# Sliding-window attention and a gated layer on one core: attention rewritten in blocks of 32 queries by 64 keys

## The chip, the core and the metric

One NeuronCore of a Trainium2 chip runs the whole program. Its engines work in parallel and meet through semaphores: TensorE (PE in the profile; PEld are its weight loads) for matmuls and transposes, VectorE (DVE), ScalarE (ACT), GpSimd (POOL), and SyncE (SP), from whose queue all DMA transfers between the large memory and the on-chip buffers are issued. Matmuls write into PSUM; VectorE and ScalarE read it from there. The metric is device time in microseconds (us), the median of several executions.

## What is computed

Eight batch entries, 8 heads, 576 positions, 64 features a head, all fp32. Heads 0 to 3 are "plain" (each query sees the last 32 keys), heads 4 to 7 "dilated" (every fourth key, 32 of them). The attention's output, heads side by side (512 features), goes through a gated layer with a causal convolution over 5 positions.

```python
scores = scale * np.matmul(q, k.transpose(0, 1, 3, 2))
rel = pos[:, None] - pos[None, :]
mask_plain = (rel >= 0) & (rel < 32)
mask_dil = (rel >= 0) & (rel < 32 * 4) & (rel % 4 == 0)
attn = softmax(np.where(mask, scores, -1e9))
x = np.matmul(attn, v)        # heads moved beside each other: [8, 576, 512]
for k in range(5):
    gate_pre += conv_w[k] * xp[:, k:k + S, :]
gate = 1.0 / (1.0 + np.exp(-gate_pre))
out = (gate * (x @ w_val)) @ w_out
```

## The kernel before, in words

**Who sets the order.** Every piece of work is a `Task` with an engine, an assumed duration, the tasks it depends on, and the buffers it needs (`Ten`). `Plan.run` simulates the engines on these durations and emits the instructions in the order it finds: at each step the task that could start first, and among equals the one with the lowest priority number. A batch b has priority b for dilated attention, b + 0.45 for plain, b + `lag` (1.171) for the gated stages; `TUNE["kind"]` shifts each kind. Loads go out strictly in the order of their priorities and wait there for a free buffer. A waiting instruction holds back all that stands behind it on its engine.

**Dilated attention** (`dilated`, heads in two pairs y). One load each brings q and k for the four heads: 96 partitions of 12 rows (3 KB) per head pair (`load_qk`, L340). v comes with 4 positions a partition, twice for some of them: `va` 128 partitions, `vb` the last 64 (L363, L368); GpSimd casts both to bf16 (L386). Six transposes per operand (L548) bring features onto partitions, where two heads lie in the two halves; VectorE and ScalarE evict them (L557, L382, L384). Scores are matmuls of 64 keys by up to 126 queries in quadrants of the array (L577), in two halves cb. The exponential is on ScalarE (L394), the mask multiply on VectorE (L407). Attention times v is 4 matmuls of full height (L588) and 4 of 64 by 32 (L596). A column of ones beside v gives the row sums; the reciprocal (L606) and the multiply (L607) normalise. Transposes (L616, L619) bring the result back, and a copy puts it into `xT` (L382 on ScalarE, L384 on VectorE).

**Plain attention** (`plain`) does the same with 48 transposes of 96 columns per batch (24 for q, 24 for k; L430), score matmuls of 64 keys by 96 queries (L463), attention times v on 128 rows of `et` (L476), normalising (L486, L487) and transposes (L496). Its v is loaded in overlapping windows of 128 rows each 96 rows (L348, L354), in packets of 256 B, so that a third of v is read twice.

**Gated stages** (`gated`) per batch, in two halves of 288 positions and two pairs of chunks: the convolution as 20 matmuls of 64 by 64 with diagonal weights (L647), tanh on ScalarE (L657), the value product as 8 matmuls (L665), and their product on VectorE (L675) into `y_all`. **Outputs**: 36 blocks of 128 rows, each 4 matmuls of 512 columns (L692), an eviction (L700 on ScalarE, L702 on VectorE) and a store (L706).

The weights come through `va` buffers after the first loads (L750); GpSimd casts them (L762, L772). PSUM has three tiles of two banks (`ps2`, shown as pd) and two of one bank (`ps1`, shown as pu).

```python
key = (at, t.prio, s + dur)
if best is None or key < best[0]:
    best = (key, t, eng, dur, s)
```

Of the kernel before, what the change touches and what calls it, by code (L numbers as in the profile page):

```python
# [2 lines left out]

# [8 lines left out]
ALU = mybir.AluOpType  # L12
# [4 lines left out]
TUNE = {'seed': 108242,  # L17
 'jit': 0,
 'lag': 1.171,
 'plain': 0.45,  # L20
 'unit': 0.056,
 'half': 0.406,
 'chunk': 0,
 'look': {'PE': 0.0, 'ACT': 0.081, 'DVE': 0.05, 'POOL': 0.309, 'SP': 0.02},
 'flex': 0.712,
 'switch': 0.047,
 'kind': {'V': 0.708,
          'Sp': -0.063,
          'EXp': 0.259,
          'Y': -0.322,  # L30
          'Td': 0.582,
          'Md': -0.23,
          'Ct': 0.552,
          'Cd': 1.11,
          'Ed': 0.138,
          'Np': -0.673,
          'Qd': -0.751,
          'early': -0.369,
          'Kd': -0.627,
          'Ap': 0.43,  # L40
          'EXd': 0.163,
          'ST': -0.388,
          'EKp': 0.363,
          'Wv': -0.368,
          'Mp': -0.254,
          'Ep': 1.186,
          'Nd': 0.592,
          'Wo': -0.345,
          'Ad': 0.079,
          'TQp': 0.323,  # L50
          'TKp': -0.445,
          'Xp': 0.531,
          'EQp': -0.504,
          'Sd': -0.045,
          'G': -0.497,
          'Xd': -0.432,
          'EO': 0.659,
          'C': 0.303,
          'O': -0.056}}
# [39 lines left out]
class Plan:  # L99
# [15 lines left out]
    def add(self, *a, **k):  # L115
        t = Task(*a, **k)
        kind = t.name.rstrip("0123456789")
# [84 lines left out]
def kernel(  # L202
# [17 lines left out]
    W = 32  # L220
    PB = 12
    NP = S // PB
    TT = S // R
    NCH = Dm // 128
    NB = S // 96
# [4 lines left out]
    PM = 42  # L230
    M1, M2 = 3 * PM, 3 * (NP - PM)
    K1 = TT - 128
    scale = 1.0 / float(D) ** 0.5
    HEADS = [[0, 2], [1, 3], [4, 5], [6, 7]]
    VHEADS = [0, 2, 3, 1, 4, 5, 7, 6]

    N = {"ps2": 3, "ps1": 2, "qk": 8, "vp": 2, "va": 3, "vb": 2, "vab": 2, "vbb": 2,
         "qTp": 1, "kTp": 3, "qTd": 2, "kTd": 2, "et": 4, "xn": 3, "gate": 3, "osb": 5, "avt": 2}
# [10 lines left out]
    qk = tiles("qk", [96, 2, PB * D], FP32)  # L249
    vp = tiles("vp", [128, 4, NB, DA], FP32)  # L250
    va = tiles("va", [128, 4, R * D], FP32)
    vb = tiles("vb", [128, 4, R * D], FP32)
    vab = tiles("vab", [128, 4, R, DA], BF16)
    vbb = tiles("vbb", [128, 4, R, DA], BF16)
    qTp = tiles("qTp", [128, PB, 2, NP], BF16)
    kTp = tiles("kTp", [128, 32 + S], BF16)
    qTd = tiles("qTd", [128, 2, 3, 2, NP], BF16)
    kTd = tiles("kTd", [128, 2, 2, TT], BF16)
    et = tiles("et", [128, 2 * HW + 32], BF16)
    xn = tiles("xn", [128, 6, 2, D], BF16)  # L260
    gate = tiles("gate", [128, 2, HW], BF16)
    osb = tiles("osb", [128, Dm], FP32)
    rec = consts.tile([128, 2, 12], FP32, name="rec")

    xT = consts.tile([128, NCH, B * SB], BF16, name="xT")
    y_all = consts.tile([128, NCH, NTOK], BF16, name="y_all")
    ident = consts.tile([128, 128], BF16, name="ident")
    ident2 = consts.tile([128, D], BF16, name="ident2")
    ident_f = consts.tile([8, 8], FP32, name="ident_f")
    perm_p = consts.tile([96, 96], BF16, name="perm_p")  # L270
    perm_m = consts.tile([M1, M1], BF16, name="perm_m")
    perm_r = consts.tile([128, R, 32], BF16, name="perm_r")
    mask_d = consts.tile([128, HW], BF16, name="mask_d")
    mask_p = consts.tile([128, 96], BF16, name="mask_p")
# [7 lines left out]


    def early():
# [3 lines left out]
        nc.vector.memset(mask_d, 1.0)  # L288
        m1 = mask_d[:, 0:2 * M1].rearrange("p (x s t) -> p x s t", x=2, s=3)
        m2 = mask_d[:, 2 * M1:].rearrange("p (x s t) -> p x s t", x=2, s=3)  # L290
        for m, n, b in ((m1, PM, 0), (m2, NP - PM, M1 - K1)):
            band(m, b, [[0, 2], [1, 3], [3, n]])
        nc.vector.memset(mask_p, 1.0)
        band(mask_p.rearrange("p (r t) -> p r t", r=PB), 32, [[1, PB], [PB, 8]])
        for x in vab + vbb:
            nc.vector.memset(x[:, :, :, D:DA], 1.0)
        for x in et:
            nc.vector.memset(x[:, 2 * HW:], 1.0)
        for x in kTp:
            nc.vector.memset(x[:, 0:32], 0.0)  # L300
        for x in vp:
            nc.vector.memset(x[0:32, :, 0, :], 0.0)
            nc.vector.memset(x[:, :, 1:NB, D:DA], 1.0 - 2.0 ** -9)
            nc.vector.memset(x[32:64, :, 0, D:DA], 1.0 - 2.0 ** -9)
            nc.vector.memset(x[64:128, :, 0, D:DA], 1.0 - 2.0 ** -9)
# [3 lines left out]
        nc.vector.tensor_copy(perm_p.rearrange("p (t r) -> p t r", r=PB),  # L309
                              ident[0:96, 0:96].rearrange("p (r t) -> p t r", r=PB))  # L310
        nc.vector.tensor_copy(perm_m.rearrange("p (t s) -> p t s", s=3),
                              ident[0:M1, 0:M1].rearrange("p (s t) -> p t s", s=3))
        nc.vector.tensor_copy(perm_r, ident.rearrange("p (c n) -> p c n", c=R))
        nc.vector.tensor_copy(
            perm_r[:, :, 32 - M2:].rearrange("p c (t s) -> p c t s", s=3),
            ident.rearrange("p (c n) -> p c n", c=R)[:, :, 32 - M2:].rearrange("p c (s t) -> p c t s", s=3))
        nc.vector.memset(
            xT.rearrange("z c (b t) -> z c b t", b=B)[:, :, :, 0:4], 0.0)

    def band(dst, base, pattern):  # L320
        nc.gpsimd.affine_select(out=dst, in_=dst, compare_op=ALU.is_ge, fill=0.0,
                                base=base, pattern=pattern, channel_multiplier=-1)
        nc.gpsimd.affine_select(out=dst, in_=dst, compare_op=ALU.is_ge, fill=0.0,
                                base=W - 1 - base,
                                pattern=[[-a, n] for a, n in pattern],
                                channel_multiplier=1)
# [9 lines left out]
    def load_qk(src, b, dil, y, ten, prio):  # L336
        ys = range(2) if y is None else [y]

        def issue():
            nc.sync.dma_start(  # L340
                out=qk[ten.idx][:, ys[0]:ys[-1] + 1, :],
                in_=src_ap(src, (b * H + 4 * dil + 2 * ys[0]) * S * D,
                           [[PB * D, 96], [2 * S * D, len(ys)], [1, PB * D]]))
        return load(f"qk{b}{dil}", ten, issue, 0.78 * len(ys), prio)

    def load_vp(b, ten, prio):
        def first():
            nc.sync.dma_start(  # L348
                out=vp[ten.idx][32:128, :, 0, 0:D],
                in_=src_ap(v, b * H * S * D, [[D, 96], [S * D, 4], [1, D]]))  # L350
        res = [load(f"vp{b}", ten, first, 0.43, prio)]
        for h in range(4):
            def rest(h=h):
                nc.sync.dma_start(  # L354
                    out=vp[ten.idx][:, h, 1:NB, 0:D],
                    in_=src_ap(v, (b * H + h) * S * D + 64 * D,
                               [[D, 128], [96 * D, NB - 1], [1, D]]))
            res.append(load(f"vp{b}{h}", ten, rest, 0.72, prio))
        return res

    def load_vd(b, ta, tb, prio):
        def first():
            nc.sync.dma_start(  # L363
                out=va[ta.idx],
                in_=src_ap(v, (b * H + 4) * S * D, [[R * D, 128], [S * D, 4], [1, R * D]]))

        def second():
            nc.sync.dma_start(  # L368
                out=vb[tb.idx][64:128],
                in_=src_ap(v, (b * H + 4) * S * D + (TT - 64) * R * D,  # L370
                           [[R * D, 64], [S * D, 4], [1, R * D]]))
        return (load(f"va{b}", ta, first, 1.5, prio), load(f"vb{b}", tb, second, 0.8, prio))


    def score_mm(o, lhs, rhs, lane):
        for m in range(2):
            nc.tensor.matmul(out=o[64 * m:64 * m + 64], lhsT=lhs[:, 64 * m:64 * m + 64],
# [437 lines left out]
```

## Time and profile before

| | |
|---|---|
| Median of 3 runs | 205.73 us (204.80 to 207.56) |
| The profiled execution's span | 206.9 us |
| PE, VectorE, ScalarE, GpSimd busy | 165.9, 121.0, 102.4, 33.2 us |
| Mean granted clock of TensorE | 0.922 |
| Read from and written to the large memory | 33.30 MB, 9.44 MB |
| DMA packets | 43687, of them 25731 under 512 B |

The profile is one execution; its span is the time from the first to the last instruction, and no other time of that execution is recorded. "Busy" is the union of an engine's instructions. Matmuls are pipelined, so a row's mean duration of one matmul holds latency, and many of them overlap; the time of a group in the chain of waits, or from its start to the next group's start, is a better price. The granted clock is the share of full speed that TensorE was given. A line such as L577 is a line of the kernel's file; where a helper records the instruction, several tiles share a line.

### The profile page before, as it was taken

To read this page: it belongs to the slowest core of one execution; us is meant where nothing else is said; L and a number is where in the kernel's file an instruction comes from. 1 tells how busy PE (TensorE), PEld (TensorE's weight loads), DVE (VectorE), ACT (ScalarE), POOL (GpSimd) and SP (SyncE) were. 2 spreads that over 40 slices of the span, in tenths; PEclk is the share of its full clock that TensorE was granted. 3 is DMA by queue.
4 is the path that set the end of the run, shared out by engine and by line. 5 is a ranking of instruction groups with operands and counts; after the bars stand their busy time and mean duration, and the time that the engine had idled before them with its cause. 6 is when DMAs were issued, how large, how long until landed. Compare 5 with 4: busy or idle time off the path is not lost.

```text
span 206.9 us, 7180 instructions
## 1 busy us (share of the span) xinstructions
PE 165.9 (80%) x3117; PEld 121.9 (59%) x3140; DVE 121.0 (58%) x239; ACT 102.4 (49%) x170; POOL 33.2 (16%) x52
## 2 busy tenths in 40 slices
PE   1278955992898787949995999599996999999992
PEld 1166834662677665637673767387664766676650
DVE  6165651551597775728874668448665577785320
ACT  2315711451657564742482278552674547846443
POOL 5300272400350040004000340440040000000000
PEclk9999998896559999999999799959997999999998
DMA  6999859999999999999999999999998512202205
GB/s 181 238 230 213 200 157 271 260 198 254 309 282 228 245 220 144 228 257 250 300 258 239 288 244 283 223 272 260 242 310 134 208 51 105 106 3 105 101 34 219
DMA packets 43687, 43.20 MB, mean 209 GB/s; under 512 B 25731, under 2 KB 31880, under 8 KB 43656
## 3 DMA queue, kind: packets, MB, share of 16 engines
q1 hardware_dynamic: 43656, 42.75, 85.2%
q8 instruction: 24, 0.39, 0.9%
q14 instruction: 7, 0.06, 0.1%
HBM read 33.30 MB, written 9.44 MB: 207 GB/s over the span
## 4 chain that ended last, share of the span: by engine, by line
PE 61%; DMA 21%; issue 7%; SPq 4%; DVE 3%; ACT 1%; POOL 1%; ACTq 0%; POOLq 0%; DVEq 0%
DMA qk<-in_k_dram 15%; PE pu L692 14%; PE pd L665 13%; PE pd L647 10%; PE pu L548 4%; PE pd L430 3%; DMA va<-in_moe_w_val_dram 3%; PE pd L476 3%; DMA qk<-in_q_dram 3%; PE pd L577 2%; PE pd L588 2%; SPq L354 2%; PE pd L596 2%; PE pd L463 2%; PE pu L496 2%
## 5 line engine op out<-in xcount | busy, mean ns | idle before, releaser
L394 ACT ACTIVATE et<-pd 128x576 bf16<-128x576 f32 x64 | 38.2, 649 | 29.3 <-PE pd L577 16.6
L665 PE MATMUL pd<-xT,w_val 128*128 128x288 bf16 x256 | 38.0, 295 | 0.5 <-DVE xT L384 0.5
L692 PE MATMUL pu<-w_out,y_all 128*128 128x512 bf16 x121 | 33.0, 380 | 2.0 <-issue 1.1
L657 ACT ACTIVATE gate<-pd 128x576 bf16<-128x576 f32 x32 | 20.5, 652 | 22.8 <-PE pd L647 22.8
L675 DVE SCALAR_TENSOR_TENSOR y_all<-gate,pd 128x576 bf16<-128x576 bf16 x32 | 23.8, 750 | 13.7 <-PE pd L665 13.2
L647 PE MATMUL pd<-xT,conv_diag 64*64 64x288 bf16 x640 | 28.6, 328 | 3.6 <-issue 3.1
L548 PE MATMUL pu<-ident,qk 96*128 96x96 bf16 x192 | 16.0, 236 | 17.0 <-DMA qk<-in_q_dram 16.5
L665 PEld LDWEIGHTS <-w_val 128*128 128x128 bf16 x256 | 24.2, 101 | 7.4 <-POOL w_val L762 0.9
L647 PEld LDWEIGHTS <-conv_diag 64*64 64x64 bf16 x640 | 22.0, 124 | 6.7 <-issue 5.0
L548 PEld LDWEIGHTS <-qk 96*128 96x128 bf16 x192 | 12.0, 113 | 20.3 <-DMA qk<-in_q_dram 17.1
L386 POOL CAST vab<-va 128x1024 bf16<-128x1024 f32 x8 | 8.3, 1040 | 95.1 <-DMA va<-in_v_dram 63.7
L382 ACT COPY xT<-pu 128x576 bf16<-128x576 bf16 x20 | 12.8, 642 | 21.5 <-PE pu L619 15.4
L700 ACT ACTIVATE osb<-pu 128x512 f32<-128x512 f32 x26 | 15.5, 598 | 10.9 <-PE pu L692 9.7
L692 PEld LDWEIGHTS <-y_all 128*128 128x128 bf16 x144 | 12.2, 98 | 13.4 <-issue 1.2
L407 DVE TENSOR_TENSOR et<-et,mask_d 128x576 bf16<-128x576 bf16 x32 | 14.9, 469 | 8.8 <-ACT et L394 8.1
L407 DVE TENSOR_TENSOR et<-et,mask_p 128x576 bf16<-128x576 bf16 x29 | 16.0, 560 | 6.2 <-ACT et L394 5.5
L487 DVE TENSOR_TENSOR xn<-pd,rec 96x768 bf16<-96x768 f32 x16 | 15.3, 954 | 0.6
L557 DVE COPY qTd<-pu 128x576 bf16<-128x576 bf16 x16 | 7.2, 453 | 12.2 <-PE pu L548 12.2
L382 ACT COPY kTd<-pu 128x576 bf16<-128x576 bf16 x12 | 7.7, 638 | 13.0 <-PE pu L548 13.0
L463 PE MATMUL pd<-qTp,kTp 64*64 64x96 bf16 x384 | 10.3, 227 | 4.2 <-issue 3.7
L607 DVE TENSOR_TENSOR xn<-pd,rec 128x640 bf16<-128x640 f32 x16 | 13.2, 824 | 0.5
L430 PE MATMUL pd<-ident,qk 96*64 96x96 bf16 x384 | 11.0, 216 | 2.7 <-DMA qk<-in_k_dram 1.4
(62 smaller groups left out, 185.1 us busy)
## 6 DMA issues: line engine op xcount, KB each, us to landing
out_dram<-osb SPq DMA_DIRECT2D x36, 256.0 KB, 4.7
qk<-in_q_dram SPq DMA_DIRECT2D x15, 576.0 KB, 7.7
qk<-in_k_dram SPq DMA_DIRECT2D x15, 576.0 KB, 9.8
vp<-in_v_dram SPq DMA_DIRECT2D x32, 160.0 KB, 7.7
va<-in_v_dram SPq DMA_DIRECT2D x8, 512.0 KB, 9.5
vb<-in_v_dram SPq DMA_DIRECT2D x8, 256.0 KB, 10.0
va<-in_moe_w_val_dram SPq DMA_DIRECT2D x4, 256.0 KB, 7.2
va<-in_moe_w_out_dram SPq DMA_DIRECT2D x4, 256.0 KB, 6.5
```

The source lines that it names most:

```text
L382: nc.scalar.copy(out=out_, in_=in_)
L394: nc.scalar.activation(out=et[e.idx][:, 0:2 * HW].rearrange("p (l n) -> p l n", l=2), in_=ps2[ps.idx][:, :, 0:HW], func=AF.Exp, scale=scale)
L407: nc.vector.tensor_tensor(out=ev, in0=ev, in1=m, op=ALU.mult)
L430: nc.tensor.transpose(out=o[64 * y:64 * y + 64, r // 3, (r % 3) * 96:(r % 3) * 96 + 96], in_=a[:, y, r * D:(r + 1) * D], identity=ident[0: ...
L487: nc.vector.tensor_tensor(out=xn[xt.idx][0:96].rearrange("p (h j) l d -> p h (j l) d", h=2), in0=a[:, :, :, 0:D], in1=rr[:, :, :, None].to ...
L548: nc.tensor.transpose(out=o[:, (cb * 3 + s) * 96:(cb * 3 + s + 1) * 96], in_=a[:, y, c:c + 128], identity=ident[0:96, 0:96])
L647: nc.tensor.matmul(out=ps2[pc.idx][64 * ob:64 * ob + 64, n, 0:HW], lhsT=conv_diag[rb, 2 * cp + n, kk, :], rhs=xT[rb, 2 * cp + n, s:s + HW] ...
L657: nc.scalar.activation(out=gate[g.idx], in_=ps2[pc.idx][:, :, 0:HW], func=AF.Tanh, scale=0.5)
L665: nc.tensor.matmul(out=ps2[pv.idx][:, n, 0:HW], lhsT=w_val[:, mc, c * 128:(c + 1) * 128], rhs=xT[:, mc, c0:c0 + HW], start=(mc == 0), stop ...
L675: nc.vector.scalar_tensor_tensor(out=y_all[:, 2 * cp:2 * cp + 2, t0:t0 + HW], in0=gate[g.idx], scalar=1.0, in1=ps2[pv.idx][:, :, 0:HW], op ...
L692: nc.tensor.matmul(out=ps1[po.idx], lhsT=y_all[:, c, t0:t0 + 128], rhs=w_out[:, c, :], start=(c == 0), stop=(c == NCH - 1))
L700: nc.scalar.activation(out=osb[ob.idx], in_=ps1[po.idx], func=AF.Copy, scale=0.5)
```

## The change

All heads now go through one function, `attend`, for two heads at a time (four units a batch): 18 blocks of 32 queries by 64 keys (the block's own 32 positions and the 32 before them), for two heads 36 score matmuls, one exponential and one mask multiply over 640 columns, 36 products with v of 64 rows by 32 columns of the array, one normalisation. For the dilated heads a position's four phases are treated as four sequences, of which a unit takes two.

Loads: q and k of the plain heads lie over 128 partitions with 9 rows (2304 B) each, those of the dilated heads with 4 rows (1 KB); v is loaded once, plain in rows of 256 B, dilated in 1 KB. Blocks that start in the middle of a 64-row piece need v shifted by 32 partitions. GpSimd makes that copy (`vs`) in four instructions of 32 partitions, and for the dilated heads an unshifted cast (`vn`). Odd blocks read `vp` or `vn`, even ones `vs`. Transposes back write 64-partition halves of PSUM.

`xT` becomes 4 rotating buffers of one batch, `y_all` 3 rotating buffers of two batches. The planner's constants are new: `lag` 4.106, `plain` 0.442, jitter 0.264 on every priority, other shifts per kind (k loads -1.7 to -1.0, v loads +0.5 and -0.6, w_val load at 0.524 + 0.858, w_out load at 5.256 + 1.13), and 9 `qk` buffers. The gated stages and outputs compute the same as before.

```diff
-TUNE = {'seed': 108242,
- 'lag': 1.171,
+TUNE = {'seed': 283419,
+ 'jit': 0.264,
+ 'lag': 4.106,
+ 'wv': 0.524,
+ 'wo': 5.256,
...
-                in_=src_ap(src, (b * H + 4 * dil + 2 * ys[0]) * S * D,
-                           [[PB * D, 96], [2 * S * D, len(ys)], [1, PB * D]]))
+                in_=src_ap(src, b * H * S * D, [[PJ * D, 128], [2 * S * D, 2], [1, PJ * D]]))
...
+            nc.sync.dma_start(out=t[:, 0:4, :], in_=src_ap(src, o, [[RD, 128], [128 * RD, 4], [1, RD]]))
...
+            nc.sync.dma_start(out=t[0:64, 4, :], in_=src_ap(src, o + 512 * RD, [[RD, 64], [1, RD]]))
...
-                    out=vp[ten.idx][:, h, 1:NB, 0:D],
-                    in_=src_ap(v, (b * H + h) * S * D + 64 * D,
-                               [[D, 128], [96 * D, NB - 1], [1, D]]))
+            nc.sync.dma_start(out=vp[ten.idx][:, :, 0:D],
+                              in_=src_ap(v, b * H * S * D, [[D, 128], [128 * D, 18], [1, D]]))
...
+    def attend(name, b, u, s, qt, kt, deps, v_odd, v_even, v_deps, v_tens, prio):
+        ps, e, po, xt = Ten("ps2"), Ten("et"), Ten("ps2"), Ten("xn")
+
+        def sc(eng):
+            for g in range(NG):
+                h, blk = place(g, s)
+                for l in range(2):
+                    rb = slice(64 * l, 64 * l + 64)
+                    nc.tensor.matmul(
+                        out=ps2[ps.idx][64 * h:64 * h + 64, l, 32 * blk:32 * blk + 32],
+                        lhsT=kT[kt.idx][rb, 32 * g:32 * g + 64],
+                        rhs=qT[qt.idx][rb, 32 * g:32 * g + 32], start=True, stop=True)
...
+            nc.scalar.activation(out=et[e.idx], in_=ps2[ps.idx][:, :, 0:EW], func=AF.Exp, scale=scale)
...
+            nc.vector.tensor_tensor(out=et[e.idx], in0=et[e.idx], in1=m, op=ALU.mult)
...
+                        nc.tensor.matmul(
+                            out=ps2[po.idx][32 * c:32 * c + 32, h, n * DA:(n + 1) * DA],
+                            lhsT=et[e.idx][64 * h:64 * h + 64, l, 32 * blk:32 * blk + 32],
+                            rhs=src(p, l)[64 * h:64 * h + 64], start=True, stop=True,
+                            tile_position=(64 * h, 32 * c))
+        t_a = plan.add(f"A{name}", {PE: 0.30}, avm, deps=[t_m] + v_deps, tens=[e, po, xt] + v_tens,
+                       prio=prio, mode="6432")
...
+                if i == 0:
+                    copy(eng, vs[ts.idx][0:32, 1:18, 0:D], vp[tv.idx][96:128, 0:17, 0:D])
+                else:
+                    copy(eng, vs[ts.idx][a:a + 32, 0:18, 0:D], vp[tv.idx][z:z + 32, :, 0:D])
+            sh.append(plan.add(f"W{b}", {POOL: 1.2}, cv, deps=lv, tens=[tv, ts], prio=prio))
...
+                            nc.tensor.transpose(
+                                out=o[64 * y:64 * y + 64, PR * j:PR * j + PR],
+                                in_=a[rb, (y * PJ + j) * D:(y * PJ + j + 1) * D], identity=ident2[rb, :])
...
+        def nat(eng):
+            copy(eng, vn[tn.idx][:, 0:16, 0:D], vd[tv.idx].rearrange("p c (n x) -> p (c n) x", n=R)[:, 0:16])
+            copy(eng, vn[tn.idx][0:64, 16:20, 0:D], vd[tv.idx].rearrange("p c (n x) -> p (c n) x", n=R)[0:64, 16:20])
+        sh.append(plan.add(f"U{b}", {POOL: 1.4}, nat, deps=lv, tens=[tv, tn], prio=prio))
```

More of the change, by code (lines that the diff above doesn't have):

```diff
@@ L2 @@
 from contextlib import ExitStack
+from itertools import takewhile
 import concourse.bass as bass
@@ L14 @@
 PE, ACT, DVE, POOL, SP = "PE", "ACT", "DVE", "POOL", "SP"
-TUNE = {'seed': 108242,
- 'jit': 0,
- 'lag': 1.171,
[L20 to L59, printed above, removed]
+TUNE = {'seed': 283419,
+ 'jit': 0.264,
+ 'lag': 4.106,
+ 'plain': 0.442,
+ 'unit': -0.05,
+ 'half': -0.304,
+ 'chunk': 0.171,
+ 'look': {'PE': 0, 'ACT': 0.014, 'DVE': 0, 'POOL': 0.804, 'SP': 0.792},
+ 'flex': 0.058,
+ 'switch': 0.083,
+ 'conv': 0.109,
+ 'wv': 0.524,
+ 'wo': 5.256,
+ 'bufs': {'ps2': 3,
+          'ps1': 2,
+          'qk': 9,
+          'vp': 2,
+          'vd': 2,
+          'vn': 2,
+          'vs': 4,
+          'qT': 4,
+          'kT': 4,
+          'et': 4,
+          'xn': 4,
+          'gate': 3,
+          'osb': 5,
+          'xT': 4,
+          'yT': 3},
+ 'kind': {'Y': 0.742,
+          'Ap': -5.466,
+          'G': 2.013,
+          'Nd': 2.485,
+          'Fp': -0.2,
+          'Cd': 3.289,
+          'Lwv': 0.858,
+          'Lc': -0.724,
+          'Fd': -1.043,
+          'Sd': 0.441,
+          'EO': 1.34,
+          'Wo': 0.159,
+          'U': -1.299,
+          'Lwo': 1.13,
+          'Xd': -0.142,
+          'Ekd': -4.439,
+          'Md': -0.853,
+          'Ad': -1.988,
+          'Sp': -0.665,
+          'Xp': -1.215,
+          'Lkr': -1.69,
+          'Lvp': -0.616,
+          'Ekp': -1.147,
+          'Ed': 2.938,
+          'Eqd': -0.076,
+          'Wv': -1.214,
+          'Eqp': 1.365,
+          'Ep': -2.267,
+          'Np': -1.538,
+          'Tqp': -0.912,
+          'Lvd': 0.523,
+          'Tqd': -1.554,
+          'early': 1.836,
+          'Lkd': -1.276,
+          'V': -0.187,
+          'Ct': -3.598,
+          'Lkp': -0.958,
+          'ST': -0.371,
+          'Tkd': -0.913,
+          'W': 2.23,
+          'O': 1.356,
+          'Mp': 0.057,
+          'Lqp': -0.49,
+          'Lqd': 0.396,
+          'Tkp': 3.231,
+          'C': -0.141,
+          'Lvr': 0.691,
+          'Lqr': 0.195}}
@@ L611, in dilated @@
-            t_n = plan.add(f"Nd{b}{y}", {DVE: 1.05}, norm, deps=t_av, tens=[po, xt, at], prio=p)
-            def trx(eng, xt=xt, psx=psx):
-                o = ps1[psx.idx].bitcast(BF16)[:, 0:S].rearrange("p (c t) -> p c t", c=R)
-                xx = xn[xt.idx].rearrange("p n x d -> p n (x d)")
-                nc.tensor.matmul(out=o[:, :, TT - 32:TT], lhsT=xx[:, 4, :], rhs=perm_r,
-                                 is_transpose=True, start=True, stop=True)
-                for c in range(R):
-                    nc.tensor.transpose(out=o[:, c, 0:M1], in_=xx[0:M1, c, :], identity=perm_m)
```

585 lines of the change are left out of this document (263 added, 322 removed).

## The prediction, made before the changed kernel was run

> **What bounds the kernel now.** I read the page first (busy shares, slices), then the table of windows, the chain of waits in order of time, and last the rows of single lines. Batch b below is one of the 8 batch entries, "gated" the stages behind attention (conv, val, their product), "output" the last matmul.
>
> ```profile
> span 206.9 us, 7180 instructions
> ...
> PE 165.9 (80%) x3117; PEld 121.9 (59%) x3140; DVE 121.0 (58%) x239; ACT 102.4 (49%) x170; POOL 33.2 (16%) x52
> ...
> PE   1278955992898787949995999599996999999992
> ...
> PEclk9999998896559999999999799959997999999998
> DMA  6999859999999999999999999999998512202205
> ```
>
> The lines of digits are 40 slices of 5.2 us: the transfers (DMA) are full for 31 slices and nearly idle after. So there are two resources near their limit up to 160 us, and one after. The windows give it in numbers (busy us of each engine, then clock, DMA share, GB/s):
>
> ```profile
> 0.00:40.00 40.00, 24.64 (x426) 19.11 (x430) 19.33 (x59) 12.87 (x20) 13.01 (x34) 0.96 0.92 217
> 40.00:160.00 120.00, 99.18 (x2015) 73.81 (x2027) 76.70 (x138) 64.65 (x108) 20.16 (x19) 0.89 1.07 247
> 160.00:207.00 47.00, 42.12 (x700) 28.94 (x699) 25.00 (x44) 24.87 (x42) 0.00 (x0) 0.97 0.28 103
> ```
>
> PE is idle 15.4 us in the first stage, 20.8 in the second, 4.9 in the third: 41.1 of 206.9. The second stage is also where the granted clock is lowest (0.89). The chain (start, duration, what) says what the idle time is made of:
>
> ```profile
> 3.58 8.36 DMA qk<-in_k_dram
> 17.55 6.77 DMA va<-in_moe_w_val_dram
> 45.11 7.55 DMA qk<-in_k_dram
> 63.60 1.14 PE pd L430 x48
> 67.18 14.86 DMA qk<-in_k_dram
> 85.02 0.45 PE pd L577 x28
> 86.72 0.38 PE pd L463 x24
> 87.71 3.12 issue
> 94.03 0.48 PE pd L476 x12
> 146.80 0.36 PE pu L548 x6
> ```
>
> Between 45 and 82 us two k loads stand on the chain for 22.4 us. Elsewhere PE work of 0.4 to 2 us hands over to PE work. So: PE's own work is the bound, and late loads add to it. The PE rows also price small matmuls: 48 transposes take 1.14 us, 24 score matmuls 0.38, 12 attention-times-v matmuls 0.48.
>
> The last view is that of the mask multiply and of the GpSimd casts (minimum/median/maximum ns):
>
> ```profile
> L407 DVE TENSOR_TENSOR et<-et,mask_d x32: 443/458/925, 7.6 to 178.7; 128x576 bf16<-128x576 bf16 x32
> L407 DVE TENSOR_TENSOR et<-et,mask_p x29: 445/458/1373, 21.0 to 187.0; 128x576 bf16<-128x576 bf16 x29
> ...
> L386 POOL CAST vab<-va x8: 1038/1040/1043, 8.6 to 152.3; 128x1024 bf16<-128x1024 f32 x8
> L386 POOL CAST vbb<-vb x8: 1041/1042/1266, 9.8 to 153.4; 64x1024 bf16<-64x1024 f32 x8
> ```
>
> A mask takes 458 ns, and up to 1373 where it meets a GpSimd instruction.
>
> **The change part by part.** The sum is made against the profiled execution's span, 206.9 us; it is 1.2 us (0.6%) above the median 205.73, inside 204.80 to 207.56.
>
> Transfers. Read bytes go from 33.30 MB to q, k, v once (3 x 9.44) and weights 2.10: 30.4 MB. Writes stay 9.44. By the trace's packets, time over 16 engines: 6144 of 3072 B at 198 ns (76.0 us), 6149 of 1024 B at 73 (27.9), 23572 of 256 B at 25 (36.2), 5632 of 2048 B at 98 (34.5), semaphores 1.6, instructions 2.1; sum 178. After: 4096 of 2304 B (plain q and k, 128 partitions), 13824 of 1024 B, 18432 of 256 B, the same 2048 B. A 2304 B packet over 128 partitions is not in the trace. At the rate of 3072 B over 96 it is 149 ns, at that of the 2048 B stores in the tail (86 ns) it is 97; I take 120, nearer the loads. The 1024 B packets took 58 to 74 ns into 128 partitions (va, batch by batch) and 78 to 98 into 64 (vb); I take 65. Sum 30.7 + 56.2 + 28.8 + 34.5 + 3.7 = 154 us; bounds 142 and 170. Less the stores (26) and the weights (8), that is 120 us for 8 batches: one lands each 15 us.
>
> PE. Gated and output are unchanged: per batch 4 x (0.61 + 0.98), and 36 outputs of 4 x 0.216, 82 us in all at full clock. Attention per batch before, from the chain's and timeline's rows: plain transposes 1.14, dilated 4 x 0.36, scores 2 x 0.38 + 2 x 0.45, attention times v 2 x 0.49 + 4 x 0.40, back transposes 2 x 0.36 + 2 x 0.50: 8.5 us. With 82 that is 150, and 150/0.92 (mean clock) 163, against 165.9 busy: the rows add up. After, per batch:
> - Plain transposes: 72 of 64 columns in place of 48 of 96. L430 runs at 21.4 ns each; scaled by columns 14.3. So 1.0 to 1.5, I take 1.25.
> - Dilated transposes: 20 in place of 24, 128 columns in place of 96: 1.2 to 1.44, I take 1.44.
> - Scores: 144 (32 queries by 64 keys) in place of 112. L463 and L577 run at 14 to 16 ns with their tails, 10.7 without; the 18-column half of L577 gains less than its columns. 1.5 (10.7) to 3.1 (21.4, the start to start of L430, where two halves of the array take turns), I take 2.0 by L577.
> - Attention times v: 144 of 64 x 32 in place of 56. L596, the one 64 x 32 form, starts every 14 ns: 2.0; low 1.5, high 3.1 by the same two rows.
> - Back transposes: 60 of 128 to 64 in place of 22: at 54 ns for 128 columns, two at a time, 0.35 x 2 + 0.62 x 2 = 1.9; 1.65 to 2.4.
> Sum 8.6, low 6.9, high 11.5. Against 8.5 that is nothing; bounds -13 and +24 us over 8 batches. More instructions, but smaller and packed. The term in the sum is 0.
>
> [...]
>
> ScalarE and VectorE. Exponentials: 64 x 649 ns to 32 of 640 columns, 721 ns: -15 us. Masks 64 to 32, 509 each: 31 to 16. Normalising: 32 x (824 + 219) against 35.6: -2. Copies out of PSUM: 88 (54 us) to 96 at some 0.62: +6. The two stand at 223 us of 414 before and at some 198 after. They are off the path; the term is 0. Score tiles leave PSUM sooner: 16 pairs of banks per batch in place of 22.
>
> GpSimd. Per batch: four shifted copies of plain v (3 x 1152 and 1088 elements a partition), four of dilated v (3 x 1024 and 1280) and an unshifted cast (1280), 10.2 k elements at 1.016 ns (the 1024 in 1040 ns): 10.3 us, 83 over the kernel, where 17.0 were. No row moves data between partitions: the low end is this row, the high end 2.1 ns per element (the select of L323, 1.21 us for 576), 21.4 us per batch. I take the cast, which is the same operation. Its cover is PE's pace, (8.6 + 6.4)/0.92 = 16 us per batch. The attention-times-v step waits for it now, and behind that wait on PE stand the next tasks in program order.
>
> Masks against GpSimd. The 61 masks lost 3.3 us over 458 ns while GpSimd was 16% busy: 0.34 us each per full share. With GpSimd at 0.75 in the loading stage that is 0.26 each, 8 us on VectorE, which brings the two engines to 206: hidden, bounds 0 and 32 x 1.0.
> [...]
>
> Order. q and k loads, the weights and stores all pass through SP: 9 loads a batch in place of 11. k is loaded ahead of q by some 1.7 batches, so the first complete batch comes after some 2.9 MB, at about 15 us (plain scores were at 19.7). w_val comes after some 2.4 batches, cast at about 42 us (28.6 before); w_out after some 6.6 batches, near 105 us, where the first output ran at 40.2. Outputs are held until then: six batches of y have buffers, and it is the same 34 us of PE work, done later, while reads have the queue alone. I cost this at 0 in the sum, but if w_out were later than 120 us the 31 us of outputs and the last gated work would not be covered by any attention. At the start I take idle 17 in place of 15.4: +1.5.
>
> Where the stall goes. Idle in 40 to 160 was 20.8. A batch lands each 15 us and takes PE 16, so most waits for k go; the next late things are v's copies and the exponential behind a score. I leave 9 of 20.8: -12 (bounds -19 and 0). Clock: 0.71 in 40 to 60 and 0.84 in 120 to 140 lost 4 + 3 us; half comes back with the gaps gone: -3.5 (0 to -7). Tail: the same 3.6 us after the last matmul.
>
> Sum: 206.9 + 0 - 12 - 3.5 + 1.5 = 193; on the scale of the median 192.
>
> **The rivals.**
> First, cheaper small matmuls: attention at the low end, 6.9 per batch, takes 13 more: 179. For: L463 unstalled at 10.7 ns. Against: tails of 0.1 to 0.2 us at each change of shape, as L588 to L596.
> Second, the loads gain and PE gives it back: attention at 10.0 per batch, half way to the high end, is +12: 204. For: twice the small matmuls. Against: L596's 14 ns.
> Third, GpSimd becomes the bound, the other side. Place: the attention-times-v step of each half batch. It starts near 14 us, needs 8 x, 6 us of weights, then the last batch's attention and gated work (16) and the end (4). At 2.1 ns per element x is 21.4: 211. It decides from x = 19 us (1.87 ns per element). [...] Against: both casts at 1.04 us.
> Fourth, attention at the high end, small matmuls at L430's 21.4 ns: +24: 216. For: successive score blocks share a quadrant. Against: 10.7 to 16 ns in the rows of quadrant matmuls. [...]
>
> **How the numbers follow.** Forecast 0.46 (183 to 201 by itself), first rival 0.16, second 0.15, third 0.13, fourth 0.10. 2% is about what a measurement of this kernel can tell: under 201.6 is faster, over 209.8 slower. Faster: nearly all of the forecast, the first, a fifth of the second: 0.64. Same: the rest of the forecast and most of the second: 0.10. Slower: third, fourth, a fifth of the second: 0.26. The range 174 to 216 leaves out the lowest of the first, the upper part of the third and half of the fourth, some 0.13.
>
> **What would show it.** Right: DMA time near 154 us (share 0.8 of a 192 us span) with reads done by 130; PE busy 160 to 168; idle in the middle under 10; GpSimd some 90 busy, a copy of 1024 at 1.04; masks mostly over 0.51 until the loads end; outputs only after about 105 us. Wrong: a shifted copy over 1.9 us, PE waiting for GpSimd on the chain; scores of 36 over 0.7 us; DMA share unchanged.

## The result, and the profile after

The changed kernel takes 234.35 us (median of 4 runs, 231.01 to 236.04) where the kernel before took 206.64 beside it on the same chip (204.80 to 210.45): a ratio of 1.125, 95% interval 1.110 to 1.140. The forecast was 192 (174 to 216). The profiled execution of the changed kernel took 236.04 us with a span of 234.3; it is one of the longer ones (the shortest took 231.01), and the accounting below is of it.

Page of the changed kernel: busy shares, slices of 5.9 us, queues.

```profile
span 234.3 us, 10001 instructions
...
PE 176.4 (75%) x4564; PEld 130.1 (56%) x4564; DVE 107.4 (46%) x210; ACT 98.6 (42%) x159; POOL 91.3 (39%) x107
...
PE   0352747898695958984795699099789889999993
PEclk9999999999978897999589779769999999999999
DMA  4999999844977930399009897502004404614155
...
q1 hardware_dynamic: 43880, 39.86, 57.6%
q8 instruction: 35, 0.57, 1.0%
```

The loads need less, as was forecast: the row of transfers, full for 31 slices before, has holes from the ninth slice on. VectorE, ScalarE and GpSimd are all under half busy. And yet PE is busy for a smaller share (75% where it was 80%), with holes that no other row fills. The windows of the changed kernel put numbers to it (busy of each engine, clock, DMA share, GB/s):

```profile
0.00:40.00 40.00, 17.43 (x573) 14.02 (x577) 21.13 (x66) 11.02 (x17) 20.59 (x39) 1.00 0.98 265
40.00:160.00 120.00, 92.38 (x2778) 73.01 (x2771) 60.47 (x101) 50.55 (x82) 69.85 (x68) 0.87 0.61 170
160.00:234.30 74.30, 66.62 (x1221) 43.10 (x1219) 25.76 (x44) 37.04 (x61) 0.85 (x1) 1.00 0.34 128
```

PE's idle time in the three stages is 22.6, 27.6 and 7.7 us, against 15.4, 20.8 and 4.9 before: 16.8 more. Its busy time is 10.5 more (176.4 against 165.9). Together that is the 27.4 us between the two spans. The chain of waits of the changed kernel names what the idle time waits for:

```profile
19.61 3.41 issue
31.76 4.74 issue
...
61.07 2.27 issue
...
71.58 2.51 issue
...
83.47 2.72 issue
...
109.20 3.81 issue
...
125.96 2.45 issue
...
146.86 5.72 issue
```

"Issue" is time in which the engine waited for nothing that the profile shows: no semaphore, no transfer of the kernel's, no other engine. It is 17.4% of the chain, the largest entry, where it was 7.1% before (the longest ones are shown). The stop at 109.20 stands in the middle of a task, as the timeline of PE shows (start, time to the end of the last, line, tile, matmuls):

```profile
108.93 0.20 PE L446 MATMUL pd<-vs,et 64*32 64x65 bf16 x2
...
109.01 0.19 PE L446 MATMUL pd<-vn,et 64*32 64x65 bf16 x1
113.01 0.23 PE L446 MATMUL pd<-vn,et 64*32 64x65 bf16 x1 [3.81 <-issue]
113.02 0.24 PE L446 MATMUL pd<-vs,et 64*32 64x65 bf16 x2
```

Some 19 of one task's 36 products start within 0.1 us, PE stands still for 3.8, and the others follow. Both parts read the same tiles, so no tile can have been late. When PE's instructions are counted from the start, matmuls and weight loads together, the stops fall on round numbers. My count of the trace of the changed kernel:

```
stop at us       19.61 27.14 31.76 42.37 61.07 71.58 83.47 109.20 125.96 167.48 190.03
instructions so far 446  702   958  1214  2238  2750  3262   4796   5564   7355   8379
minus 190, / 256      1    2     3     4     8    10    12  17.99  20.99  27.99  31.99
```

(A few records are missing from the trace, hence 17.99.) The queue called "instruction" carries packets of 16384 bytes; 256 instructions lie between two such boundaries, and 35 packets for PE's 9128 instructions fit that. So a packet is 256 instructions; I call it a code page. At 109.20 PE stops, the next packet starts at 110.33 and takes 1.08 us, and PE goes on 1.6 us after its end. Before, PE had 6280 instructions (3140 weight loads and as many matmuls, of which 3117 are in the trace) and 24 packets.

From 19 us on all 17 stops of over 0.5 us stand at such a boundary, 38.5 us in all; in the kernel before 5 do, 10.9 us. (This is my sum over the traces, between the first and the last matmul; "stops for code" below are these.) PE's other gaps fell from 21.8 to 9.9 us, and its busy time rose by 10.5. So the stops for code, 27.6 us more, are as much as the whole loss of 27.4; the other two changes nearly cancel.

The packet list also tells why a page is late. By the stops, a packet brings the page that begins 1.3 to 1.6 us after its end. In the changed kernel 32 of the 35 packets start 1.0 us or more after PE has begun the page before that one (the three others from 0.4 us ahead to 0.8 behind), also after pages that lasted 8 to 15 us and left time to spare. So in this trace code came one page ahead at most: 1.0 us to the packet's start, 1.1 for the packet and 1.4 until PE went on make some 3.5 us from page to page, and a page used up sooner ended in a stop.

### The profile page after: what moved, and what is told of

Its sections match the earlier page's. It is cut to its first block, busy times and chain, and to the rows that moved or that the text cites. A ratio compares the mean times of both kernels' runs of the same rounds, so it can differ in the third digit from the quotient of the medians.

```text
span 234.3 us, 10001 instructions
## 1 busy us (share of the span) xinstructions
PE 176.4 (75%) x4564; PEld 130.1 (56%) x4564; DVE 107.4 (46%) x210; ACT 98.6 (42%) x159; POOL 91.3 (39%) x107
## 4 chain that ended last, share of the span: by engine, by line
PE 70%; issue 17%; DMA 6%; DVE 4%; ACT 1%; SPq 0%; DVEq 0%; ACTq 0%
PE pd L664 15%; PE pu L692 13%; PE pd L646 10%; PE pu L617 7%; PE pu L584 7%; PE pd L419 6%; PE pd L446 5%; PE pu L495 4%; DMA qk<-in_q_dram 4%; PE pu L524 3%; DVE et L431 2%; DMA qk<-in_k_dram 2%; DVE kT L403 1%; DVE yT L674 1%; PE pu L526 0%
## 5 line engine op out<-in xcount | busy, mean ns | idle before, releaser
L405 POOL CAST vs<-vp 32x1152 bf16<-32x1152 f32 (+1 forms) x32 | 36.4, 1141 | 27.0 <-DMA vp<-in_v_dram 25.6
L674 DVE SCALAR_TENSOR_TENSOR yT<-gate,pd 128x576 bf16<-128x576 bf16 x32 | 23.9, 753 | 42.0 <-PE pd L664 42.0
L405 POOL CAST vs<-vd 32x1024 bf16<-32x1024 f32 (+1 forms) x32 | 35.5, 1111 | 1.7
L692 PE MATMUL pu<-w_out,yT 128*128 128x512 bf16 x144 | 33.2, 379 | 0.0
L700 ACT ACTIVATE osb<-pu 128x512 f32<-128x512 f32 x36 | 21.5, 597 | 27.4 <-PE pu L692 27.4
L584 PE MATMUL pu<-ident,qk 128*128 128x128 bf16 (+1 forms) x160 | 19.7, 248 | 9.7 <-DMA qk<-in_k_dram 5.6
L495 PE MATMUL pu<-ident,qk 64*64 64x64 bf16 x576 | 15.7, 209 | 13.2 <-issue 10.4
L426 ACT ACTIVATE et<-pd 128x640 bf16<-128x640 f32 x32 | 21.6, 709 | 7.9 <-PE pd L419 7.8
L431 DVE TENSOR_TENSOR et<-et,mask 128x640 bf16<-128x640 bf16 x32 | 20.8, 670 | 4.3 <-ACT et L426 4.3
L692 PEld LDWEIGHTS <-yT 128*128 128x128 bf16 x144 | 13.8, 97 | 15.3 <-issue 1.4
L495 PEld LDWEIGHTS <-qk 64*64 64x64 bf16 x576 | 13.5, 123 | 14.2 <-issue 12.0
```

Source lines behind the costliest of these rows:

```text
L405: nc.gpsimd.tensor_copy(out_, in_)
L426: nc.scalar.activation(out=et[e.idx], in_=ps2[ps.idx][:, :, 0:EW], func=AF.Exp, scale=scale)
L431: nc.vector.tensor_tensor(out=et[e.idx], in0=et[e.idx], in1=m, op=ALU.mult)
L495: nc.tensor.transpose(out=o[64 * y:64 * y + 64, PR * j:PR * j + PR], in_=a[rb, (y * PJ + j) * D:(y * PJ + j + 1) * D], identity=ident2[rb, :])
L584: nc.tensor.transpose(out=o[:, 128 * c:128 * c + m], in_=a[0:m, c * RD + 128 * cb:c * RD + 128 * cb + 128], identity=ident[0:m, 0:m])
L674: nc.vector.scalar_tensor_tensor(out=yT[yb.idx][:, 2 * cp:2 * cp + 2, t0:t0 + HW], in0=gate[g.idx], scalar=1.0, in1=ps2[pv.idx][:, :, 0:HW ...
```

## The experiments

Theory C: PE waits for its own code. In the changed kernel's trace two packets of code start 3.34 us apart or more, 256 instructions of small matmuls are used up in 1 to 2 us (an estimate from its chain, where the 72 of a unit's products take 0.34 us and those of its scores 0.42), and the change raised PE's instructions from 6280 to 9128. Rivals: L, the loads come late, because the load queue stands behind plain v's buffer (54.5 us in 5 waits on the queue of SP); G, GpSimd's copies hold products up or lengthen the masks on VectorE (482 ns at the median, up to 1537); P, the outputs come too late (the first at 157 us), so that nothing covers their stage. Several kernels leave part of the computation out; the expectations say which. Ratios are to the kernel before.

**The old kernel with more instructions.** Same mathematics, same columns: conv and value matmuls cut in two, the output matmul in four.

```diff
-for kk in range(K):
-    for n in range(2):
-        for hb in range(2):
+for z, kk, n, hb in [(z, kk, n, hb) for z in (0, 144) for kk in range(K)
+                     for n in range(2) for hb in range(2)]:
...
-for mc in range(NCH):
+for z, mc in [(z, mc) for z in (0, 144) for mc in range(NCH)]:
...
-for c in range(NCH):
+for z, c in [(z, c) for z in range(0, 512, 128) for c in range(NCH)]:
```

> The kernel before, same results, but its wide matmuls are cut: convolution and value product in 2 pieces of 144 columns, output in 4 of 128. The array streams the same columns; PE's instructions (matmuls and weight loads) go from 6275 to 8931, about as many as the changed kernel's 9123. Theory C (PE waits for its own code at the end of each page of 256 instructions, 16 KB): 10 more pages; if every page cost what those of the changed kernel cost on average (about 2.3 us beyond cover) this gives 206 + 23 = 229 us; if only pages that are used up faster than the next arrives (some 4 us) cost, then only the convolution's 5 new pages count (128 matmuls of 15 ns, 2 us a page) and it is some 216. Theory L (loads held behind the two buffers of plain v) and theory G (GpSimd's copies): neither is in this kernel, so only the small cost of more matmuls, at most 5 us: 206 to 211.

Measured 233.58 us, ratio 1.124 (1.104 to 1.144). The old loads, the old GpSimd work and the old order of outputs, with 35 packets of code like the changed kernel, give the changed kernel's time. It is 4 us above what C had with every page at the changed kernel's price (229) and far above C's other figure (216, only the convolution's pages). The stops for code grow from 10.9 to some 29 us. The rest of the 26.7 us is not split further; the cut also doubles the weight loads of these matmuls (PEld 159.2 us busy). The page of this kernel:

```profile
span 232.4 us, 9859 instructions
...
PE 176.5 (76%) x4468; PEld 159.2 (69%) x4468; DVE 122.2 (53%) x239; ACT 102.2 (44%) x170; POOL 33.6 (14%) x52
...
q8 instruction: 35, 0.57, 1.1%
```

**The changed kernel with fewer instructions.** Scores in 4 matmuls of 320 columns per unit in place of 36 of 32, products in 8 of 325 in place of 36 of 65; loads, copies, exponentials, masks and outputs as they were.

```diff
-for g in range(NG):
-    h, blk = place(g, s)
+for h in range(2):
...
-        out=ps2[ps.idx][64 * h:64 * h + 64, l, 32 * blk:32 * blk + 32],
+        out=ps2[ps.idx][64 * h:64 * h + 64, l, 0:EW],
...
-for n in range(5):
-    for c in range(4):
-        for h in range(2):
+for c in range(4):
+    for h in range(2):
...
-            out=ps2[po.idx][32 * c:32 * c + 32, h, n * DA:(n + 1) * DA],
+        out=ps2[po.idx][32 * c:32 * c + 32, h, 0:5 * DA],
```

> The changed kernel with the same order, loads and copies, but the 36 score matmuls of a unit are replaced by 4 of 320 columns and the 36 products by 8 of 325 columns, so the attention's result is left out. PE's instructions go from 9123 to 5283. The array's time falls by some 0.2 us a unit for the scores and 0.1 for the products, about 8 us in all. Theory C: 15 pages fewer, and the bursts that use up a page in 1 to 2 us are gone: 232 - 8 - 25 = 195 to 205 us, gaps of over 0.6 us after a 256th instruction from 38 us to under 10. Theory L and theory G: loads, buffers and copies are as they were, so 222 to 228.

Measured 192.69 us, ratio 0.935 (0.928 to 0.942): 41.7 us less than the changed kernel, with every other part of the change in place, and below C's own range (195 to 205).

```profile
span 191.3 us, 6147 instructions
...
PE   0236899799996869987999929998999999999992
PEclk9999999969999999996999996999999999999999
...
q8 instruction: 20, 0.33, 0.7%
```

PE's row is nearly full from the fifth slice on, the clock hardly dips (0.971 in the mean), and "issue" is 2% of its chain. Not all of the 41.7 us is code, though: PE's busy time times its clock is 155 us here and 165 in the changed kernel, so up to some 10 us may be the array's own time, and the difference is an upper bound for the code's part.

**Half of that.** Only the products made wide (the second half of the diff above).

> The kernel after, in which only the value products of a unit are made wide: 8 matmuls in place of 36, and each with its weight load, so PE's instructions fall from 9123 to 7331 and their code by 7 pages of 256. The products' result is then not the reference's; everything else runs as it was. Theory C (PE waits for its own code): between the kernel after (234 us) and the one with both kinds wide (192.7), at about 212 to 218 us, since 15 pages fewer took 41.7 us away and 7 pages should take some 20. Theory L (the loads) and theory G (GpSimd's copies): neither is touched, 229 to 234 us less at most 3 us of array time.

Measured 211.51 us, ratio 1.017 (1.007 to 1.028), half a microsecond under C's range: 22.8 us less for 7 code pages less (28 packets), where 15 took 41.7. In these kernels time goes with the number of code pages, at 3.3 and 2.8 us each (upper bounds, as above); in the old kernel cut small it is 26.7 us for 11 more, 2.4 each.

**Code alone.** The old kernel, with 1024 small matmuls appended, where neither loads nor other engines do anything but the last stores.

```diff
+    for i in range(256):
+        for m in range(2):
+            for l in range(2):
+                rb = slice(64 * l, 64 * l + 64)
+                nc.tensor.matmul(out=ps1[l][64 * m:64 * m + 64, 0:32], lhsT=w_val[rb, 0, 64 * m:64 * m + 64],
+                                 rhs=w_out[rb, 0, 0:32], start=True, stop=True)
```

> The kernel before with 1024 matmuls of 64 by 64 by 32 columns (2048 PE instructions, 8 pages of code) at its end, when hardly a transfer runs; they feed nothing. This measures the disputed cost by itself. If PE is bound by the array, the rows of such matmuls (9 ns each) give 9 us: 215 us. Theory C with a page arriving each 3.6 us (the shortest distance between two code packets in the changed kernel) gives 8 x 3.6 = 29 us less one or two pages already there: 228 to 235, and the matmuls run in bursts of 128 with a wait after each.

Measured 233.98 us, ratio 1.122 (1.104 to 1.141). (Two code packets of the changed kernel are 3.34 us apart at the least; 3.6 is near the next ones, 3.54 to 3.65.) The timeline of PE in that tail:

```profile
206.90 1.29 PE L788 MATMUL pu<-w_out,w_val 64*64 64x32 bf16 x128 [2.87 <-issue]
210.35 1.90 PE L788 MATMUL pu<-w_out,w_val 64*64 64x32 bf16 x128 [2.17 <-issue]
214.36 1.90 PE L788 MATMUL pu<-w_out,w_val 64*64 64x32 bf16 x128 [2.10 <-issue]
218.08 1.90 PE L788 MATMUL pu<-w_out,w_val 64*64 64x32 bf16 x128 [1.83 <-issue]
```

Bursts of exactly 128 matmuls, which with their weight loads are 256 instructions, start each 3.5 to 4.0 us, and between them PE waits for "issue" alone. This is the mechanism without anything that could stand in for it. The windows of the same tail give the granted clock there, 0.59:

```profile
203.00:231.20 28.20, 13.43 (x1002) 12.57 (x989) 0.00 (x0) 0.00 (x0) 0.00 (x0) 0.59 0.06 18
```

**The same tail with eight times the columns.** 256 columns in place of 32, the same 2048 instructions.

```diff
-                nc.tensor.matmul(out=ps1[l][64 * m:64 * m + 64, 0:32], lhsT=w_val[rb, 0, 64 * m:64 * m + 64],
-                                 rhs=w_out[rb, 0, 0:32], start=True, stop=True)
+                nc.tensor.matmul(out=ps1[l][64 * m:64 * m + 64, 0:256], lhsT=w_val[rb, 0, 64 * m:64 * m + 64],
+                                 rhs=w_out[rb, 0, 0:256], start=True, stop=True)
```

> The kernel before with the same 1024 extra matmuls of 64 x 64 of the array at its end, now with 256 columns each in place of 32 (their results are not used; the reference's outputs are still computed). Eight times the columns, the same 2048 instructions and 8 pages of code. A conv matmul of 288 columns in the same form costs 98 to 104 ns of a task for four that run together (20 in 1.97 to 2.54 us), so 256 columns are some 24 ns from start to start, or 3.0 us per page of 128. Theory C (a page arrives each 3.5 to 4 us whatever the matmuls do, and work goes on meanwhile): the 32-column kernel's time within 5 us, 230 to 239 us, with stops of 0.5 us or so in place of 1.6 to 2.9. Rival (each page costs a stop of some 2 us on top of its work): 206 + 8 x (3.0 + 2) = 246 us or more.

Measured 234.27 us, ratio 1.128 (1.114 to 1.142): the same time for eight times the work. Its timeline and its windows over the tail:

```profile
202.64 28.76 PE L788 MATMUL pu<-w_out,w_val 64*64 64x256 bf16 x1024 [0.73 <-ACT osb L700]
```
```profile
203.00:232.30 29.30, 28.32 (x1020) 27.38 (x1009) 0.00 (x0) 0.00 (x0) 0.00 (x0) 1.00 0.05 17
```

One burst, no gap in it of over 0.3 us, full clock: 28.76 / 8 = 3.6 us per code page. Code arrived while PE worked: with 3.6 us of work to a page, its supply cost nothing that shows beside that work. The rival (a stop on top of each one's work) falls. The columns set the pace here: four matmuls start each 109 ns (27 ns a matmul where 24 was expected), and five page boundaries pass without a jump. But that pace, 3.5 us a page, is also that of the code, so this run lies just where the two meet; with 32 columns the code sets it.

**Without GpSimd's shifted copies.** The 64 casts into `vs` are left out, and even blocks read the unshifted v.

```diff
             def cv(eng):
+                return
...
-                return lambda pp, l: vs[ts.idx][:, (9 * (x + 2 * l) + pp) // 2, :]
+                return v_odd()
```

> The changed kernel without the 64 shifted copies: GpSimd does only the unshifted cast and the weights, and even blocks read the unshifted v (the attention's result is left out). Order and all other instructions are the same. Theory G (attention times v waits for GpSimd, masks are blocked by it): 72 us of GpSimd work gone, masks back to 0.5 us, 205 to 215 us. Theory L: plain v's buffers come free sooner, the loads' waits (54 us in five waits) halve: 212 to 222. Theory C: PE's code gaps stay at 35 to 40 us: 225 to 232.

Measured 231.43 us, ratio 1.122 (1.110 to 1.134). Some 70 us of GpSimd's work gone, for about 1% between the medians. G falls.

**Four buffers for plain v.**

```diff
-    vp = tiles("vp", [128, 18, DA], FP32)
+    vp = [consts.tile([128, 18, DA], FP32, name=f"vp{i}") for i in range(4)]
...
-            nc.sync.dma_start(out=vp[ten.idx][:, :, 0:D],
+            nc.sync.dma_start(out=vp[b % 4][:, :, 0:D],
```

> The changed kernel with four buffers for plain v in place of two; same order of instructions on every engine, same results. Theory L: the five waits of the load queue for plain v's buffer (54 us) go, DMA has no holes up to 110 us, reads end 25 us sooner: 205 to 215 us. Theory C: loads come sooner, the code gaps of PE stay near 38 us: 222 to 232. Theory G: 225 to 232.

Measured 228.04 us, ratio 1.109 (1.096 to 1.122). The 54.5 us that SP's queue waited ahead of that load are gone (its loads wait for other buffers now, at most 8.7 us at a time) and the reads end at 132 us in place of 153, for 6 us between the medians (3 by the ratios). L falls as the main cause: "issue" is still 16.5% of the chain.

**Weights and outputs early.** The planner writes the order anew.

```diff
- 'wo': 5.256,
+ 'wo': 0.6,
...
-          'O': 1.356,
+          'O': -2.6,
```

> The changed kernel with w_out's load early (priority 0.6 in place of 5.256) and the outputs' priority shift -2.6 in place of 1.356; same results, and the planner puts the order together anew. Theory P (outputs are held until w_out at 137 us, while PE has idle time, and 36 of them stand in the tail): the tail of 70 us after the last load shrinks, 212 to 220 us. Theory C: outputs and other wide matmuls between bursts of small ones let a page of code last longer, gaps after a 256th instruction from 32 us to 20 or less, 215 to 222. If the place of the outputs doesn't matter: 228 to 234.

Measured 236.05 us, ratio 1.132 (1.120 to 1.144). The first output runs at 64 us in place of 157 and nothing is won. P falls. Theory C had expected a gain here as well (215 to 222, from outputs between the bursts); that was wrong too, the stops for code are still some 37 us.

**Both together**: the last two diffs in one kernel.

> The changed kernel with early w_out and early outputs (as in the run of that edit alone) and four buffers for plain v; same results. If the two gains add: 4 us below that run, 208 to 218. Theory C: still above the kernel before (206), as PE's code is as long as it was.

Measured 237.59 us, ratio 1.123 (1.105 to 1.140). Lifting both limits at once gives no more than lifting one: neither was the limit (208 to 218 was expected if the two gains add).

**Almost no transfers.** Each buffer is loaded only at its first use, later batches compute on old data.

```diff
+    loaded = set()
...
+            if again("qk", ten, "p"):
+                return
```

> The changed kernel with each buffer of q, k and v loaded only at its first use, so later batches compute on old data (results left out); same order and instructions on PE. It asks what the transfers add to the code gaps. If code packets stand behind data packets, the gaps after some 45 us shrink from 3.2 us on average to about 1.5, their sum from 32 to some 15, and waits for loads go too: 195 to 208 us. If a page's arrival is a fixed time, gaps stay near 3 us each: 215 to 225.

Measured 208.16 us in a single run, at the upper end of the range for code that stands behind data (195 to 208). Same instructions, same 35 packets of code:

```profile
PE 164.8 (80%) x4564; PEld 123.1 (60%) x4564; DVE 112.0 (54%) x210; ACT 98.7 (48%) x159; POOL 92.5 (45%) x107
...
PEclk9999999999999969999999999999999999999999
```

The stops for code fall from 38.5 to 21.0 us, PE's other gaps do not (9.9 and 11.0). So the wait for code was longer with the transfers here. The packet itself takes as long as before (1.1 us); it starts later: over 2 us after the first instruction of the page before in 14 of 35 cases with the loads, in 5 of 35 here. Which part of the transfers does it (the queue, the memory, the engines) was not tried. And the same matmuls are busy for 164.8 us in place of 176.4 at a mean clock of 0.992 in place of 0.934: so much of PE's busy time goes with the clock. It does not explain the growth over the kernel before, whose clock was lower (0.922): busy time times clock was 153 us there and is 163 to 165 in both of these. As busy time also holds the latency behind each burst of matmuls (a score matmul, L419, is listed with 172 ns or more, at 0.42 us for 36), this is a rough measure, and what the 10 us are was not separated.

**What loads and copies cost once code is out of the way.** Two of the edits above, made in the kernel with wide scores and products: no shifted copies, and four buffers of plain v.

> The kernel with wide scores and products (192.7 us; the attention's result is left out), without the 64 shifted copies on GpSimd too: even blocks read the unshifted v, which leaves out the shift. It asks what GpSimd's copies cost when the code is no longer the limit. [...] Copies hidden: 188 to 193 us.

Measured 191.88 us (median of 4 runs, 188.08 to 193.15, without an interval) against 192.69 with them. The lowest run is 4.2 us below the lowest with copies (192.31), so the copies cost between nothing and some 4 us here; these runs leave it open.

> The kernel with wide scores and products (192.7 us; the attention's result is left out), with four buffers for the plain v in place of two. It asks what the load queue's wait for a plain v buffer costs when the code is no longer the limit. Theory L (loads come late because the queue stands behind the plain v): 180 to 187 us. Wait hidden: 190 to 193 us.

Measured 187.50 us, ratio 0.894 (0.881 to 0.908) against 0.935 with two buffers. It ends just above L's range (180 to 187) and below the range for a hidden wait. The load queue's wait costs some 5 us (8 by the ratios) with the code out of the way, where it cost 6 (3) with it: a real cost in both, and a small one beside the code's.

None of these kernels that computes the reference beats the one before. What the runs point to is a kernel with these loads and the old, larger score and product matmuls, which is another rewrite and was not made.

## Why the prediction was wrong

The step that failed is the term for PE's attention: "More instructions, but smaller and packed. The term in the sum is 0." I priced matmuls by columns and by starts, and the number of instructions not at all.

- Prices of the small matmuls: right in their sum. Chain of waits of the changed kernel: transposes back of a batch's dilated heads (L617) and of a plain unit (L524), products of two units, transposes of q or k, scores of a unit:

```profile
67.71 1.77 PE pu L617 x40
...
81.04 0.68 PE pd L446 x72
81.72 0.34 PE pu L524 x8
...
94.61 0.82 PE pu L584 x10
95.43 0.42 PE pd L419 x36
95.85 0.32 PE pu L495 x18
```

Scores and products are 0.42 and 0.34 us per 36, where I had taken 0.50 each. The dilated heads' transposes cost more: 1.77 us back (1.24 taken) and 1.64 for q and k (1.44). With 1.28 for plain q and k and some 0.8 for plain back that is 8.5 us a batch, against 8.6 forecast and 6.9 in the first rival. So by these prices the matmuls cost what was forecast. But a task's 72 instructions, loads included, are gone in 0.34 us, a code page of 256 in 1.3 to 1.9 us (the bursts of the 32-column tail), and there the next one comes after 3.5. The second and fourth rival had PE give the gain back by matmul prices; the time came out above even the fourth (216), by a mechanism that neither of them had.
- "-12" for stalls between 40 and 160 us: measured +6.8 (27.6 against 20.8). Of the 20.8 before, 10.9 were already stops for code, which I had taken for waits on loads; the rest, 9.9, fell to 2.2. In its place came more stops for code, 25.4 us of this stage and 38.5 over the kernel. The view was there: "issue" stood at 3.12 us in the lines that I quoted of before, at 87.71, and I passed it over.
- "-3.5" for the clock: it assumed that gaps go and that half of the lost clock comes back with them, an estimate of mine that no run shows by itself. The gaps stayed, and the clock between 40 and 160 us went from 0.89 to 0.87. In the two other stages it went to 1.00 (from 0.96 and 0.97), so the mean rose from 0.922 to 0.934; PE's busy time rose by 10.5 all the same.
- "+1.5" at the start: +7.2. Three stops for code at 19.61, 27.14 and 31.76 take 9.4 us of that stage.
- Transfers: 154 us forecast with bounds 142 and 170, measured 58.7% of the span, 137.5 us, under the lower bound. The 2304-byte packet took 112 ns (120 taken), the 1024-byte one 55 (65), the 256-byte one 21 (25). The reads ended at 153 us and not by 130, after the load queue had waited 54.5 us for plain v's buffer.
- GpSimd: 83 us forecast for copies and casts, 83.8 measured; a copy of 1024 at 1.04 us as taken, the third rival (211) falls with the run without copies. Masks: 482 ns at the median, 670 in the mean, 1537 at most; forecast 509 + 260. The ten of the 32 that took over 500 ns all ran beside a GpSimd instruction, but the masks are only 2.2% of the chain.
- Outputs: from 157 us and not from 105. I had said that beyond 120 the last stage would be uncovered; the run with early outputs shows that this cost nothing here.
- Starts of small matmuls: within a task the products start 0.34 us / 36 = 9.4 ns apart (14 taken). The sustained pace of the small-matmul tail, 3.5 us / 128 = 27 ns, is that of the arriving code.

That the result lay on the slow side was in the forecast with 0.26, but on other grounds. One term more, and the trace of before would have bounded it: 11 code pages more, at the mean of the old kernel's 24 (10.9 / 24 = 0.45 us) 5 us, at the price of its three longest stops (3.1, 2.5 and 2.4 us) 26 to 34; 27.7 was measured between the medians. That the second price was the one to take is known only from the runs.

## What to carry to other kernels

Count PE's instructions, matmuls and weight loads, beside its columns: in the tail of this case 128 matmul and weight-load pairs ran once in 3.5 to 4 us, so by my estimate (3.6 us / 128, from the 256-column tail) a long stretch in which pairs would take under some 28 ns runs at the pace of its code. Cutting the old kernel's large matmuls into small ones cost 26.7 us at the same columns, and the tail took the same time with eight times the columns (233.98 and 234.27 us). In the changed kernel's trace the sign was "issue" in the middle of a task, at distances of 256 instructions, that ended 1.3 to 1.6 us behind a packet of the instruction queue.

## What the runs showed of the hardware

- The supply of code was not hidden. A packet of the instruction queue is 16384 bytes, 256 instructions by the count above; two packets never start closer than 3.3 us (changed kernel) and 3.8 (before), a packet takes 1.1 us at the median of the changed kernel (0.9 to 1.6), PE goes on 1.3 to 1.6 us after its end where it had stopped (changed kernel), and the longest stop was 5.72 us with loads under way, when the packet started 5.5 us after PE had begun the page before.
- The granted clock was low in a tail without long stops. In the tail of 32-column matmuls the stops are 1.6 to 2.9 us, PE was busy for 13.43 of 28.20 us, and the granted clock is 0.59; in the tail of 256 columns, with PE busy for 28.32 of 29.30 us, it is 1.00.
